# Loading the last rows of wo: the last 16 partitions in two loads of their own, and b1 and b2 from SyncE's queue

## The chip, the cores and the metric

The kernel runs on one core of a Trainium2 chip. The metric is device time in microseconds (us) of one execution. One execution was also recorded by the hardware profiler; its rows are what the profile sections quote.

## The reference, cut to what matters

Two tokens (B = 2) of width 512 go through one decode step of attention with cached keys and values, and through a small MLP that gates the result. K and V hold 32 heads of 8192 positions of 128 values for each token, all in fp32.

```python
def _A_ref(x, k_cache, v_cache, wq, wo):        # attention
    q = (x @ wq).reshape(B, Sq, H, Dh).transpose(0, 2, 1, 3)
    scores = einsum("bhqd,bhkd->bhqk", q, k_cache) * (Dh ** -0.5)
    o = einsum("bhqk,bhkd->bhqd", softmax(scores), v_cache)
    return o.transpose(0, 2, 1, 3).reshape(B, Sq, H * Dh) @ wo

def _B_ref(x, w1, b1, w2, b2):                  # MLP, d_ff = 1376
    h = gelu(layernorm(x) @ w1 + b1)
    return h @ w2 + b2

xn = layernorm(x)
out = x + _A_ref(xn, k, v, wq, wo) * silu(_B_ref(xn, w1, b1, w2, b2))
```

## The kernel before

**Tiling.** K and V are streamed in 32 turns. A turn takes two heads, one in partitions 0 to 63 and one in 64 to 127; each partition holds 128 positions of 128 values, so one turn's K and one turn's V are 8 MB each. VectorE multiplies K by q (`scores_mul`, L524) and sums over the 128 values (`scores_sum`, L531), each in two halves; `max_rows` and `max_dve` find the maximum, ScalarE takes the exponentials (`exps`, L552), and TensorE multiplies by V (`weighted`, L575, 64 matmuls).

**Buffers and queues.** K has two buffers (`kb0`, `kb1`), V one (`vb`). All large loads go out from SyncE, through the helper `load` (L314), on one queue, in program order: w1, w2, wq, the two halves of the first K turn, then K and V in turns, each as soon as its buffer is free. The last V turn goes into `kb1`. ScalarE issues three small loads at the start: x (L337), b1 and b2 (L339).

**Order.** `Plan` records every operation with the keys it reads and writes, and gives each engine its instructions in the order of recording, with the semaphore waits that the keys need. Every load has a semaphore of its own name (the fourth argument of `load` is the list of keys that it writes). SyncE runs no arithmetic, so its instructions are the loads in order, each behind its waits.

**The head.** While w1, w2, wq and the first K land, x is normalized twice, the MLP runs (`mlp`: L410 and L412 for w1 and b1, L452 for w2, L459 and L462 for b2), then q is computed (L482), and copied to all partitions (L495, L497). SyncE waits for L482 before it loads the second K turn into `kb0`, where wq was. b1 is one row of 1376 values in partition 32, b2 one row of 512; L412 and L462 add them with a matmul from a row of ones. w1, w2, b1, b2 and all small tiles of the head lie in `vb`, which the first V load overwrites.

**The tail.** After the last V turn that uses `vb`, `wo` is loaded there in five pieces (L619 to L621). Partition p holds 32 rows of wo, row c being 2 KB; `WO_PIECES` cuts the rows at 0, 16, 24, 29, 31 and 32, so the pieces are 4096, 2048, 1280, 512 and 256 KB over all 128 partitions. Meanwhile the last turn is finished, and `on`, the normalized attention output, is made. Then TensorE contracts: rows 0 to 23 with a 512 wide matmul each into `wide` (L648), which ScalarE copies out (L651); rows 24 to 28 with four 128 wide matmuls each into `acc` (L657, `rows(WIDE, FOLD)`); four matmuls that fold `wide` into `acc` (L662); rows 29 to 31 like 24 to 28 (`rows(FOLD, OC)`). A matmul of row c waits for the piece that holds it (`piece(c)`). `acc` is multiplied by the gate (L666), x is added (L667), and SyncE stores 4 KB (L668). WIDE is 24, FOLD 29, OC 32.

An fp32 matmul shows in the profile as two entries, each with its weight load.

Of the kernel before, what the change touches and what calls it, by code (L numbers as in the profile page):

```python
# [21 lines left out]
class Plan:  # L22
# [18 lines left out]
    def op(self, eng, fn, r=(), w=(), over=(), it=None, loop=False, dma=None):  # L41


        o = Op()
        o.eng, o.fn, o.it, o.loop, o.dma, o.tell = eng, fn, it, loop, dma, False
        need = {}

        def after(d, war):
            if d.dma is None and dma is None and d.eng == eng and (eng == "pe" or war):
                return  # L50
            if d.dma is None:
                if need.get(d.eng) is None or need[d.eng].idx < d.idx:
                    need[d.eng] = d
            else:
                k = ("dma", d.dma)
                if need.get(k) is None or need[k].idx < d.idx:
                    need[k] = d

        for k in r:
            if k in self.writer:  # L60
                after(self.writer[k], False)
        for k in list(w) + list(over):
            if k in self.writer:
                after(self.writer[k], False)
            for d in self.readers.get(k, ()):
                after(d, True)
        clock = self.clock[eng]
        need = {k: d for k, d in need.items() if clock.get(k, 0) < d.idx}
        o.deps = [(k, d) for k, d in need.items()
                  if not any(e is not d and e.done.get(k, 0) >= d.idx for e in need.values())]  # L70
        for _, d in o.deps:
            for k, v in d.done.items():
                clock[k] = max(clock.get(k, 0), v)
        own = eng if dma is None else ("dma", dma)
        self.count[own] = o.idx = self.count.get(own, 0) + 1
        o.done = dict(clock)
        o.done[own] = o.idx
        for k in w:
            self.writer[k] = o
            self.readers[k] = []  # L80
        for k in r:
            if k not in w:
                self.readers.setdefault(k, []).append(o)
        self.ops.append(o)
# [80 lines left out]
def decode_kernel(nc, x, kc, vc, wq, wo, w1, b1, w2, b2, out):  # L165
    P = 128
# [19 lines left out]
    OC = DH // PH  # L186
# [10 lines left out]
    op = plan.op  # L197

    def pe(fn, r=(), w=(), it=None, loop=False):
        op("pe", fn, r, w, it=it, loop=loop)  # L200
# [10 lines left out]
    def sbuf(name, shape):  # L211
        return nc.alloc_sbuf_tensor(name, shape, F32).ap()

    def psum(name, shape):
        return nc.alloc_psum_tensor(name, shape, F32).ap()
# [5 lines left out]
    vb = sbuf("vb", [P, KP * DH])  # L221
# [3 lines left out]
    wo_sb = vb.rearrange("p (c n) -> p c n", c=OC)  # L225
# [30 lines left out]
    on = sbuf("on", [P, RM, OC])  # L256
# [5 lines left out]
    def take(name, p, n, base=0, at=None):  # L262

        if at is None:
            at = used[0]
            used[0] += n
            assert used[0] <= KP * DH
        boot.append(name)
        return vb[base:base + p, at:at + n]
# [7 lines left out]
    b1_sb = take("b1", 1, F, R, at)  # L277
    b2_sb = take("b2", 1, D, R, at + F)
# [18 lines left out]
    acc = psum("acc", [P, P])  # L297
# [5 lines left out]
    def bank():  # L303
        i = turn[0] % 4
        turn[0] += 1
        return scratch[i], f"s{i}"
# [6 lines left out]
    def load(dst, src, sem, w, over=()):  # L313
        op("sp", lambda: nc.sync.dma_start(dst, src), (), w, over=over, dma=sem)  # L314

    def load_k(n):
        i = (n + 1) % 2
        if n in (0, N - 1):
            for s in range(2):
                load(kbuf[i][:, s * M:(s + 1) * M], kf[n][:, s * M:(s + 1) * M], f"k{i}{s}", [("kb", i, s)])  # L320
            return
        load(kbuf[i], kf[n], f"kb{i}", [("kb", i, s) for s in range(2)])
# [2 lines left out]
    WO_PIECES = (0, 16, 24, 29, 31, 32)  # L325
    WIDE, FOLD = WO_PIECES[-4:-2]


    load(w1_sb, w1.rearrange("(p c) f -> p c f", p=P), "w1", ["w1"])
    load(w2_sb, w2.rearrange("f n -> (f n)").rearrange("(p e) -> p e", p=P), "w2", ["w2"])  # L330
    load(wq_sb, wq.rearrange("(p c) n -> p c n", p=P), "wq", [("kb", 0, s) for s in range(2)])
    load_k(0)

# [1 line left out]
    dve(lambda: nc.vector.memset(eps_t, EPS), w=["eps"])  # L335
    act(lambda: nc.scalar.activation(warm, eps_t, AF.Sqrt), ["eps"], ["warm"])
    op("act", lambda: nc.scalar.dma_start(x_sb, x.rearrange("b s d -> (b s) d")), w=["x"], dma="x")  # L337
    for t, src, k in ((b1_sb, b1, "b1"), (b2_sb, b2, "b2")):
        op("act", lambda t=t, src=src: nc.scalar.dma_start(  # L339
            t.rearrange("o (k e) -> o k e", k=16), src.rearrange("(o k e) -> o k e", o=1, k=16)), w=[k], dma=k)  # L340


    pool(lambda: nc.gpsimd.memset(ident, 0.0), w=["ident"])
# [37 lines left out]
    for j in range(QT):  # L381
        pe(lambda j=j: matmul(px[R * j:R * j + RM, :P], pick, x_sb[:, j * P:(j + 1) * P],
                              start=True, stop=True), ["pick", "x"], [kx])
# [92 lines left out]
    for i in range(NQ):  # L476
        for c in range(ND):
            wv = wq_sb[:, c, :].rearrange("p (h s d) -> p h s d", s=U, d=DH)
            a = (NQ - 1 - i) * B
            for j in range(QT):  # L480
# [4 lines left out]
                    start=(i + c == 0), stop=(i == NQ - 1 and c == ND - 1)),  # L485
                   ["xnT"] + [("kb", 0, s) for s in range(2)], ["po"])
    act(lambda: nc.scalar.copy(q_nat, PO), ["po"], ["o4"])
    for k in range(N // NB):

        b, e = divmod(k, HH // NB)  # L490
        i, g = divmod(e, GQ)
        p, kp = bank()
        for s in range(U):
            a = R * (U * g + s) + B * i + b
            pe(lambda p=p, s=s, a=a: matmul(p[HP * s:HP * (s + 1), :], ident[:, a:a + 1].to_broadcast([P, HP]), q_nat,  # L495
                                            start=True, stop=True), ["ident", "o4"], [kp])
# [121 lines left out]

    wo_r = wo.rearrange("(p c) n -> p c n", p=P)  # L619
    for i, (a, e) in enumerate(zip(WO_PIECES, WO_PIECES[1:])):  # L620
        load(wo_sb[:, a:e], wo_r[:, a:e], f"wo{i}", [("wo", i)], over=["vb"])  # L621

    max_dve(N - 1)
    exps(N - 1)
# [17 lines left out]
    def piece(c):  # L642
        return ("wo", max(i for i, a in enumerate(WO_PIECES[:-1]) if a <= c))


    for c in range(WIDE):
        j = c % QT
        pe(lambda c=c, j=j: matmul(wide[R * j:R * j + RM, :], on[:, :, c], wo_sb[:, c, :],  # L648
                                   start=(c < QT), stop=(c + QT >= WIDE)), ["on", piece(c)], ["wide"])
# [4 lines left out]
    def rows(lo, hi):  # L654
        for c in range(lo, hi):
            for j in range(QT):
                pe(lambda c=c, j=j: matmul(acc[R * j:R * j + RM, :], on[:, :, c], wo_sb[:, c, j * P:(j + 1) * P],  # L657
                                           start=(c == WIDE), stop=(c == OC - 1)), ["on", piece(c)], ["acc"])

    rows(WIDE, FOLD)  # L660
    for j in range(QT):
        pe(lambda j=j: matmul(acc[R * j:R * j + RM, :], mod[:, :RM], w4[:, j * P:(j + 1) * P], start=False, stop=False),  # L662
           ["mod", "o4"], ["acc"])
    rows(FOLD, OC)

    dve(lambda: nc.vector.tensor_mul(gate, acc, gate), ["acc", "gate"], ["gate"])  # L666
# [30 lines left out]
```

## Time and profile before

| | us |
|---|---|
| median of 3 runs | 1300.4 (1300.06 to 1300.45) |
| profiled execution, its time | 1300.03 |
| profiled execution, span from first to last instruction | 1298.2 |
| VectorE busy in the span | 1134.6 (87%) |
| TensorE matmul busy in the span | 404.8 (31%) |
| DMA, mean over the span | 431 GB/s |
| TensorE clock granted, mean | 0.635 |

A core has 16 DMA engines. The DMA share of a window is the mean busy share of these 16. "issue to landing" runs from the start of SyncE's (or ScalarE's) issuing instruction to the last byte's notice on the load's semaphore. In the chain of waits each row is a start, a length and the work that the next row waited for; in the timeline a row is a start, a length, engine, line, operation, tiles and count, with the idle time before it in brackets. SPq and ACTq are the queues of SyncE and ScalarE, PEld is TensorE's weight load.

### The profile page before, as it was taken

The page shows a single profiled execution, that of the slowest core. Times are in us where ns is not written, and L with a number is a line of the kernel's source. Part 1 is how long each engine was busy: PE and PEld are TensorE (multiplying, and loading weights), DVE is VectorE, ACT ScalarE, POOL GpSimd, SP SyncE. Part 2 cuts the span into 40 slices and gives each one's busy share as a digit, 9 for nine tenths or more (in the row PEclk, how much of TensorE's full clock was granted, in tenths as well). Part 3 has the DMA queues.
Part 4 walks back from the last instruction along what each step waited for, and adds up shares of the span by engine and source line. Part 5 has one row for each costly group of instructions (what it writes and reads, how often), then busy time and mean ns, then how long its engine had stood idle before and what let it go on. Part 6 is the DMA issues. An engine that isn't in the chain of part 4 may idle for free.

```text
span 1298.2 us, 6788 instructions
## 1 busy us (share of the span) xinstructions
PE 404.8 (31%) x2728; PEld 123.9 (10%) x2728; DVE 1134.6 (87%) x276; ACT 77.6 (6%) x250; POOL 1.4 (0%) x8
## 2 busy tenths in 40 slices
PE   5602333312333312333321333321233321233337
PEld 1100011000101000101000101100001000001103
DVE  3599999888889988889988888988888988888991
ACT  1100000000000000000000000000000000000000
POOL 0000000000000000000000000000000000000000
PEclk9856666556666656666656666656666655666658
DMA  9999999999999999999999999999999999999998
GB/s 406 445 423 440 430 432 436 426 444 428 438 430 432 438 426 440 430 434 434 428 442 428 438 430 430 440 426 440 430 434 434 430 438 430 438 430 430 427 433 363
DMA packets 10826, 559.39 MB, mean 431 GB/s; under 512 B 1208, under 2 KB 1216, under 8 KB 1476
## 3 DMA queue, kind: packets, MB, share of 16 engines
q1 hardware_dynamic: 10812, 559.29, 99.7%
q8 instruction: 4, 0.07, 0.0%
q14 instruction: 2, 0.02, 0.0%
q10 hardware_dynamic: 8, 0.01, 0.0%
HBM read 559.30 MB, written 0.00 MB: 431 GB/s over the span
## 4 chain that ended last, share of the span: by engine, by line
DMA 74%; PE 24%; DVE 1%; issue 0%; ACT 0%; SPq 0%; DVEq 0%
DMA vb<-in_A_v_cache_dram 72%; PE po L575 22%; DMA vb<-in_A_wo_dram 2%; PE s L410 1%; PE po L482 1%; PE s L452 0%; PE s L412 0%; PE acc L657 0%; DVE vb L418 0%; ACT L431 0%; DVE vb L356 0%; PE s L459 0%; SPq L314 0%; DVE vb L367 0%; DVE vb L444 0%
## 5 line engine op out<-in xcount | busy, mean ns | idle before, releaser
L524 DVE TENSOR_TENSOR kb<-kb,Q 128x8192 f32<-128x8192 f32 x64 | 555.5, 8681 | 105.2 <-DMA kb<-in_A_k_cache_dram 95.9
L531 DVE TENSOR_REDUCE sc<-kb 128x64 f32<-128x8192 f32 x64 | 552.3, 8665 | 0.0
L575 PE MATMUL po<-vb,PZ 128*8 128x512 f32 x1984 | 280.7, 730 | 292.8 <-DMA vb<-in_A_v_cache_dram 292.8
L547 PE MATMUL s<-nm,srow 1*128 1x2 f32 x64 | 18.7, 359 | 364.0 <-DVE nm L541 364.0
L575 PEld LDWEIGHTS po<-vb,PZ 128*8 128x8 f32 x1984 | 56.4, 103 | 491.0 <-issue 489.5
L538 PE MATMUL s<-ident,mx 128*1 128x128 f32 x32 | 11.8, 369 | 192.7 <-DVE mx L535 192.7
L547 PEld LDWEIGHTS s<-nm,srow 1*128 1x128 f32 x64 | 15.9, 307 | 373.3 <-DVE nm L541 373.3
L582 ACT COPY o<-po 128x512 f32<-128x512 f32 x32 | 18.7, 585 | 533.3 <-PE po L575 533.3
L548 ACT COPY bias<-s 128x2 f32<-128x2 f32 x32 | 5.1, 160 | 622.1 <-PE s L547 622.1
L584 PE MATMUL s<-mod,o 128*128 128x2 f32 x256 | 33.6, 253 | 22.1 <-ACT o L582 22.1
L584 PEld LDWEIGHTS s<-mod,o 128*128 128x128 f32 x256 | 31.0, 191 | 51.3 <-ACT o L582 51.3
L552 ACT ACTIVATE PZ<-sc,bias 64x128 f32<-64x128 f32 x64 | 25.5, 399 | 1.8
L538 PEld LDWEIGHTS s<-ident,mx 128*1 128x1 f32 x32 | 2.5, 79 | 196.2 <-DVE mx L535 165.7
L590 DVE TENSOR_TENSOR Z<-blk,s 128x8 f32 (+1 forms) x32 | 5.2, 163 | 13.3 <-PE s L584 13.3
L418 DVE COPY vb<-vb 2x384 f32<-2x384 f32 x4 | 1.8, 500 | 15.9 <-ACT vb L414 15.9
L410 PE MATMUL s<-vb 128*2 128x512 f32 (+1 forms) x24 | 12.5, 673 | 0.3 <-ACT vb L375 0.3
L552 ACT ACTIVATION_READ_ACCUMULATOR PZ<-sc,bias 64x1 f32 x64 | 11.8, 185 | 0.0
L666 DVE TENSOR_TENSOR gate<-acc,gate 128x128 f32<-128x128 f32 x1 | 0.3, 291 | 12.1 <-PE acc L657 12.1
L535 DVE TENSOR_REDUCE mx<-sc 128x1 f32<-128x128 f32 x32 | 9.2, 286 | 1.1
L556 ACT ACTIVATE ZR<-half,rs 128x8 f32 (+1 forms) x32 | 9.6, 301 | 4.1
L575 PE MATMUL po<-kb,PZ 128*8 128x512 f32 x64 | 9.4, 755 | 1.4 <-ACT PZ L552 1.4
L541 DVE TENSOR_REDUCE nm<-s 1x2 f32<-1x128 f32 x32 | 8.7, 272 | 0.3 <-PE s L538 0.3
(88 smaller groups left out, 84.5 us busy)
## 6 DMA issues: line engine op xcount, KB each, us to landing
kb<-in_A_k_cache_dram SPq DMA_DIRECT2D x4, 4096.0 KB, 43.5
kb<-in_A_v_cache_dram SPq DMA_DIRECT2D x2, 4096.0 KB, 40.9
vb<-in_B_w_dram SPq DMA_DIRECT2D x2, 2752.0 KB, 12.5
vb<-in_A_wo_dram SPq DMA_DIRECT2D x1, 4096.0 KB, 19.0
vb<-in_A_wo_dram SPq DMA_DIRECT2D x1, 2048.0 KB, 23.5
vb<-in_A_wo_dram SPq DMA_DIRECT2D x1, 1280.0 KB, 26.1
vb<-in_A_wo_dram SPq DMA_DIRECT2D x1, 512.0 KB, 26.9
vb<-in_A_v_cache_dram SPq DMA_DIRECT2D x31, 29.5
```

The costliest lines, as they stand in the source:

```text
L410: pe(lambda f=f, w=w, ph=ph, c=c: matmul(ph[:B, :w], yT[:, c, :], w1_sb[:, c, f:f + w], start=(c == 0), stop=False), ["yT", "w1"], [k])
L482: pe(lambda i=i, c=c, wv=wv, a=a, j=j, hd=hd: matmul(PO[R * j:R * j + NQ * B, :].rearrange("m (h d) -> m h d", d=DH), xnT[:, c, a:a + NQ * ...
L524: vector(n, n, lambda n: nc.vector.tensor_tensor(out=k, in0=k, in1=cols(Q, n * DH, DH).unsqueeze(1).to_broadcast([P, M, DH]), op=ALU.mult) ...
L531: vector(n, n, lambda n: nc.vector.tensor_reduce(out=SC[:, s * M:(s + 1) * M], in_=k, axis=AX.X, op=ALU.add), [("kb", i, s)], [("sc", s)])
L535: vector(n, n, lambda n: nc.vector.tensor_reduce(out=MX, in_=SC, axis=AX.X, op=ALU.max), [("sc", 0), ("sc", 1)], ["mx"])
L538: pe(lambda i: transpose(PM[:1, :P], MX, ident), ["mx", "ident"], ["s1"], it=n, loop=n > 0)
L547: pe(lambda i: matmul(PN[:, :U], srow, NM, start=True, stop=True), ["srow", "nm"], ["s2"], **one)
L552: act(lambda i, r=r, s=s: nc.scalar.activation(PZ[r, :, s, :], sc[r], AF.Exp, bias=BIAS[r, s:s + 1], scale=SCALE, accum_out=RS[r]), ["bias ...
L556: act(lambda i: nc.scalar.activation(cols(ZR, i * UP - UP, UP), half, AF.Copy, scale=RS), ["half"] + [("rs", s) for s in range(U)], [("ZR" ...
L575: pe(lambda i, t=t, j=j, v=v: matmul(PO[R * j:R * j + U * JW, :], PZ[:, t].rearrange("p s j -> p (s j)"), v[:, t * JW:(t + 1) * JW, :].rea ...
L582: act(lambda i: nc.scalar.copy(O4, PO), ["po"], ["o4"], **one)
L584: pe(lambda i, k=k: matmul(PT[:, :U], O4[:, k * DH:(k + 1) * DH], mod[:, k:U * JW:JW], start=(k == 0), stop=(k == JW - 1)), ["o4", "mod"], ...
```

## The change

Rows 29 to 31 of wo (768 KB) are no longer loaded as two pieces over 128 partitions. Partitions 112 to 119 and 120 to 127 get a load each with all three rows (6 KB a partition, 48 KB a load), ahead of the two pieces, and the pieces then cover partitions 0 to 111 (448 and 224 KB). The matmuls of rows 29 to 31 wait for the two new loads as well as for their piece. The loads of b1 and b2 move from ScalarE's queue to SyncE's, behind w2 and ahead of wq.

```diff
+    PL = P - 16
     load(w1_sb, ...)
     load(w2_sb, ...)
+    for t, src, k in ((b1_sb, b1, "b1"), (b2_sb, b2, "b2")):
+        load(t.rearrange("o (k e) -> o k e", k=16), src.rearrange("(o k e) -> o k e", o=1, k=16), k, [k])
     load(wq_sb, ...)
     load_k(0)
...
     op("act", lambda: nc.scalar.dma_start(x_sb, x.rearrange("b s d -> (b s) d")), w=["x"], dma="x")
-    for t, src, k in ((b1_sb, b1, "b1"), (b2_sb, b2, "b2")):
-        op("act", lambda t=t, src=src: nc.scalar.dma_start(
-            t.rearrange("o (k e) -> o k e", k=16), src.rearrange("(o k e) -> o k e", o=1, k=16)), w=[k], dma=k)
...
     for i, (a, e) in enumerate(zip(WO_PIECES, WO_PIECES[1:])):
-        load(wo_sb[:, a:e], wo_r[:, a:e], f"wo{i}", [("wo", i)], over=["vb"])
+        if a < FOLD:
+            load(wo_sb[:, a:e], wo_r[:, a:e], f"wo{i}", [("wo", i)], over=["vb"])
+            continue
+        if a == FOLD:
+            for p in range(PL, P, 8):
+                load(wo_sb[p:p + 8, a:], wo_r[p:p + 8, a:], f"wol{p}", [("wol", p)], over=["vb"])
+        load(wo_sb[:PL, a:e], wo_r[:PL, a:e], f"wo{i}", [("wo", i)], over=["vb"])
...
-                 ... ["on", piece(c)], ["acc"])
+                 ... ["on", piece(c)] + ([("wol", p) for p in range(PL, P, 8)] if c >= FOLD else []), ["acc"])
```

More of the change, by code (lines that the diff above doesn't have):

```diff
@@ L657, in rows @@
                 pe(lambda c=c, j=j: matmul(acc[R * j:R * j + RM, :], on[:, :, c], wo_sb[:, c, j * P:(j + 1) * P],
-                                           start=(c == WIDE), stop=(c == OC - 1)), ["on", piece(c)], ["acc"])
+                                           start=(c == WIDE), stop=(c == OC - 1)), ["on", piece(c)] + ([("wol", p) for p in range(PL, P, 8)] if c >= FOLD else []), ["acc"])
     rows(WIDE, FOLD)
```

## The prediction

> **What bounds the kernel now.** I read the page's header and DMA part first, then the DMA issues with their landings, then the busy time by windows, and last the chain of waits at both ends.
>
> ```profile
> DMA 74%; PE 24%; DVE 1%; issue 0%; ACT 0%; SPq 0%; DVEq 0%
> ```
> ```profile
> q1 hardware_dynamic: 10812, 559.29, 99.7%
> q8 instruction: 4, 0.07, 0.0%
> ...
> q10 hardware_dynamic: 8, 0.01, 0.0%
> HBM read 559.30 MB, written 0.00 MB: 431 GB/s over the span
> ```
> ```profile
> 100.00:1200.00 1100.00, 314.82 (x2145) 95.93 (x2137) 1002.68 (x202) 57.39 (x197) 0.00 (x0) 0.62 1.00 434
> ```
>
> The chain by engines is three quarters DMA. SyncE's queue (q1) holds 99.7% of the 16 engines' span, and from 100 to 1200 us the DMA share is 1.00 at 434 GB/s (last two numbers of the window). So the kernel is one gapless stream of 559 MB, or 27.1 GB/s for each of 16 engines. VectorE, at 1003 of 1100 us, has spare time in every turn. A change that adds no bytes can touch only what stands before the stream and behind it.
>
> The tail is where the stream ends. The wo loads' landings come from these rows, the timeline's issues and the page's times to landing:
>
> ```profile
> 1266.34 2.23 SPq L314 DMA_DIRECT2D vb<-in_A_wo_dram  x5
> ```
> ```profile
> vb<-in_A_wo_dram SPq DMA_DIRECT2D x1, 4096.0 KB, 19.0
> vb<-in_A_wo_dram SPq DMA_DIRECT2D x1, 2048.0 KB, 23.5
> vb<-in_A_wo_dram SPq DMA_DIRECT2D x1, 1280.0 KB, 26.1
> vb<-in_A_wo_dram SPq DMA_DIRECT2D x1, 512.0 KB, 26.9
> ```
> ```profile
> vb<-in_A_wo_dram SPq DMA_DIRECT2D x1, 256.0 KB, 27.1
> ```
> ```profile
> 1266.34 0.33 SPq L314
> ...
> 1267.20 26.14 DMA vb<-in_A_wo_dram
> 1293.34 0.04 issue
> 1293.38 1.31 PE acc L657 x34
> 1294.70 0.22 PE acc L662 x7
> 1294.91 0.83 PE acc L657 x23
> 1295.75 0.02 issue
> 1295.77 0.30 DVE gate L666
> ```
>
> Five issues take 2.23 us, so the fourth and fifth start near 1267.7 and 1268.1; with 26.9 and 27.1 us the pieces land at 1294.6 and 1295.2. The chain is released by the third piece (rows 24 to 28, 1267.20 + 26.14 = 1293.34), and from there TensorE is busy nearly without a break to 1295.75. How near shows in the timeline of the same place:
>
> ```profile
> 1294.64 0.44 PEld L657 LDWEIGHTS acc<-vb,on 128*17 128x17 f32 x16
> 1294.72 0.99 PE L657 MATMUL acc<-vb,on 128*17 128x128 f32 x24
> 1295.27 0.18 PEld L657 LDWEIGHTS acc<-vb,on 128*17 128x17 f32 x8 [0.19 <-DMA vb<-in_A_wo_dram]
> ...
> 1296.42 0.70 SPq L668 DMA_DIRECT2D out_dram<-gate  x1
> ```
>
> Rows 29 and 30 load their weights from 1294.64, done at 1295.08; row 31 then stands 0.19 us idle for the last piece. So an earlier end of the stream pays at most 0.19 us, a later one pays in full.
>
> How evenly do the 16 engines finish? The last windows show it:
>
> ```profile
> 1293.25:1293.50 0.25, 0.12 (x4) 0.12 (x8) 0.00 (x0) 0.00 (x0) 0.00 (x0) 1.00 0.58 221
> 1293.50:1293.75 0.25, 0.25 (x13) 0.25 (x16) 0.00 (x0) 0.00 (x0) 0.00 (x0) 1.00 0.49 197
> 1293.75:1294.00 0.25, 0.25 (x20) 0.25 (x15) 0.00 (x0) 0.00 (x0) 0.00 (x0) 1.00 0.36 139
> 1294.00:1294.25 0.25, 0.25 (x20) 0.25 (x13) 0.00 (x0) 0.00 (x0) 0.00 (x0) 1.00 0.28 107
> ...
> 1294.50:1294.75 0.25, 0.25 (x19) 0.24 (x14) 0.00 (x0) 0.00 (x0) 0.00 (x0) 1.00 0.09 33
> ```
>
> At 1293.25 about nine of sixteen engines are still at work (0.58 x 16), at 1294.0 to 1294.25 four or five, at the end one or two. They are ragged by 1.5 us. No view names the engines.
>
> **The change part by part.** I make the sum against the profiled execution (1300.03 us; its span 1298.2 and 1.83 outside it) and add 0.37 to stand at the median of the runs, 1300.4.
>
> *Bytes per engine in the last three rows.* A piece over 128 partitions gives each engine 8 of them: 75 SyncE loads of 16 x (8 + 1) packets are 10800, and the store's 12 make the 10812 of q1. Over 112 partitions I take 7 each. For small loads the nearest row is q10's: x has two rows, b1 and b2 one each, and 8 packets fit x on two engines (2 rows, 2 end marks) and b1 and b2 on one each (1 and 1). So a load of 8 partitions goes out on 8 engines, one partition each. If both take the same eight, these carry 9 partitions of 6 KB and the others 7. 6 KB at 27.1 GB/s is 0.23 us: eight engines end 0.23 later, eight 0.23 earlier.
>
> [...]
>
> *What it does to the end.* If the last engine is among the eight with 9: row 31 waits until 1295.2 + 0.23, the end moves by +0.23. The piece with rows 29 and 30 would come 2 x 0.23 - 4 KB/27.1 (0.15) = 0.30 later, at 1294.9; its 16 weight loads (0.44) end near 1295.4, just ahead of row 31's data, so nothing more. If the last engine is among the eight with 7: its data come 0.23 earlier, and TensorE can use 0.19, unless a late engine of the other eight, four of which are late altogether, now takes the last place. Range of this term: -0.19 to +0.23.
>
> *Crowded writes.* Eight engines write into eight neighbouring partitions at once, which no row shows. Lower bound 0 (the pieces of 128 partitions run at full rate with as many engines). Upper bound: all sixteen partitions at one engine's rate, 96 KB / 27.1 GB/s = 3.6 us in place of 0.46, so +3.2 on the eight engines. I take 0, by the row of the stream that it is nearest to.
>
> *Issues and waits in the tail.* Two more issues from SyncE at 2.23 / 5 = 0.45 us put the last at 1269.5 in place of 1268.6; the first piece lands at 1285.3, so 16 us of queued data hide them. Uncovered they would cost 0.9. TensorE gets two more waits ahead of row 29, already met by then; the gaps marked issue in the chain are 0.02 to 0.04, so below 0.1 and inside the 0.19 idle. Behind them stand all of rows 29 to 31, for which L666 waits.
>
> *b1 and b2 in the head.*
>
> ```profile
> 1.47 0.53 ACTq L339 DMA_DIRECT2D vb<-in_B_b_dram  x2
> 1.65 0.43 SPq L314 DMA_DIRECT2D kb<-in_A_wq_dram  x1
> ...
> 2.12 44.65 SPq L314 DMA_DIRECT2D kb<-in_A_k_cache_dram  x3
> ...
> 17.02 1.01 PE L412 MATMUL s<-vb,ones 1*2 1x512 f32 x2
> ...
> 39.34 7.05 PE L482 MATMUL po<-kb,vb 128*4 128x512 f32 x64
> ```
> ```profile
> vb<-in_B_w_dram SPq DMA_DIRECT2D x1, 2752.0 KB, 15.5
> ```
> ```profile
> kb<-in_A_k_cache_dram SPq DMA_DIRECT2D x1, 4096.0 KB, 53.4
> ```
> ```profile
> 0.73 1.28 ACT L336 ACT_TABLE_LOAD   x1 [0.73 <-PEq L684]
> ```
>
> ScalarE's two issues (0.53 us) end at 2.00, under its table load, which ends at 2.01: their removal gives 0. On SyncE two issues of 0.27 to 0.45 us delay wq and the first K by 0.5 to 0.9 us. w1 and w2 are queued by then, and w2 (issued at 1.2, the second of two) lands at 16.7, so 13 us of data hide it. b1 now lands behind w2: 5.4 KB at 27.1 GB/s, 0.20 us, on an engine that no longer carries b1 and b2 ahead of w2's end (7.4 KB, 0.28 us). So b1 lands by 16.9 at the latest, and L412 reaches it at 17.02. I take 0. If it were late by the whole time from the store's issue (1296.42) to the end (1298.2), 1.8 us, it would land at 18.5 and TensorE would stall 1.5 us; L482 and SyncE's wait for it, which releases the second K load, slide as much. The second half of the first K, issued before 3.4 and 53.4 us under way, lands at 55.5 or later, 9 us after that load's issue (the third of its row, ending at 2.12 + 44.65 = 46.8). Cover holds; uncovered 1.5 us.
>
> **The sum**: -0.19 or +0.23 from the balance, 0 to 0.1 from waits, 0 from the rest. With both signs about as likely and the loss the larger, I take +0.1: 1300.03 + 0.1 + 0.37 = **1300.5 us**.
>
> **The rivals.**
>
> 1. *The lighter engines hold the last byte.* The forecast with the other sign, 1300.2. For it: only four or five engines are late, and they may all sit there. Against: one of four in the heavier half caps it.
> 2. *Nothing is shifted*, because the second small load takes the other eight engines: every engine keeps 8 partitions, 1300.4. For it: no row shows the engines of a small load.
> 3. *Crowded writes decide.* In full they cost 0.2 + 3.2: 1300.4 + 3.4 = 1303.8, slower by 0.26%. It passes 0.2% (2.6 us) if the 96 KB go below 96 / (2.6 - 0.23 + 0.46) = 35 GB/s together. Two partition groups in parallel give about 1302. Against: eight engines move 217 GB/s in the stream.
> 4. *Each small load holds the queue by itself.* The store shows 1.8 us for 4 KB from issue to end; two such spans give 1300.4 + 3.6 = 1304.0. Against: the last wo piece (256 KB) lands 0.6 us behind the one before, which is its bytes at 433 GB/s with no fixed time. [...]
> 5. *Instruction fetch in the tail.*
>
> ```profile
> 1294.25:1294.50 0.25, 0.25 (x17) 0.25 (x12) 0.00 (x0) 0.00 (x0) 0.00 (x0) 1.00 0.55 147
> ```
>
> The share rises again to 0.55 here, between 0.28 and 0.09: one of q8's four packets of 16 KB. With other instruction counts it can fall on an engine that still loads wo: 16 KB at 27.1 GB/s is 0.6 us, more if it is slow. 1301.0 to 1301.6.
> 6. *b1 late and the cover gone*: 1300.4 + 1.5 = 1301.9.
>
> **How the numbers follow.** Within 0.2% (2.6 us) a measurement of this kernel can't be told from no change; the three runs lie 0.39 apart. Forecast (heavier engines last) 0.39, rival 1 0.30, rival 2 0.10, rival 3 mild (about 1302) 0.06 and in full 0.02, rival 4 0.03, rival 5 0.05, rival 6 0.02. That leaves 0.03 for a cause of a gain that I don't see. Same: 0.39 + 0.30 + 0.10 + 0.06 + 0.05 + 0.02 = 0.92; slower 0.02 + 0.03 = 0.05; faster 0.03. The range takes in rivals 1 and 2 and most of 5, with the runs' scatter at both ends: 1299.9 to 1301.5. Outside are 0.02, 0.03 and 0.03 of both ends, rival 6, rival 3 mild and a little of 5, 0.17.
>
> **What would show it.** Right: q1 at 10816 packets with the loads of 48 KB on eight engines each (two pieces of 16 x 8, two loads of 16, and 4 for b1 and b2, in place of two of 144); the last landing moved by 0.2 us either way; the third piece landing unmoved against the end of V; L412 starting within 0.1 us of 17.0 and L482 within 0.2 of 39.3; the windows of the middle still at 434 GB/s. Wrong: a last piece that lands over 1 us later against the third piece (rivals 3 to 5), an idle row of L412 released by a DMA that is seen again at the issue of the second K load, or a share below 0.95 near 17 us.

## The result and the profile after

The changed kernel takes 1302.68 us (median of 22 runs, 1301.41 to 1303.56) where the kernel before takes 1300.13 (22 runs, 1300.03 to 1300.45): a ratio of 1.0017, 95% interval 1.0012 to 1.0023. It is slower by 2.55 us, just below the 0.2% that was named beforehand as indistinguishable, and outside the range of the prediction. The scatter has grown too, from 0.4 us to 2.1. The profiled execution took 1301.8 us, with a span of 1300.4.

The time divides into two parts that moved in opposite directions. Over the runs, the span rose from 1298.2 to 1301.3 us (medians of 33 runs of the kernel before and 22 of the changed one), and the time outside the span fell from 1.83 (1.87 beside the later runs) to 1.34: +3.1 - 0.5 = +2.6. The 22 spans of the changed kernel lie in two groups, ten from 1300.1 to 1300.9 us and twelve from 1301.3 to 1302.2. The profiled execution is of the shorter group, 2.2 us above the kernel before.

Page of the changed kernel, its DMA queues:

```profile
q1 hardware_dynamic: 10816, 559.30, 99.6%
q8 instruction: 4, 0.07, 0.0%
q14 instruction: 3, 0.02, 0.0%
q10 hardware_dynamic: 4, 0.00, 0.0%
```

q1 has the 10816 packets that the prediction counted: each small load is 8 packets of 6 KB and 8 end marks of 4 bytes, where a load over 128 partitions has 16 end marks. Eight engines for the one and sixteen for the other are the author's reading of these counts; no view names the engines. q14, which had two packets in the span before, has three; that row will matter below.

Windows of the changed kernel (the last two numbers are DMA share and GB/s):

```profile
100.00:1200.00 1100.00, 319.55 (x2153) 96.35 (x2141) 1001.61 (x202) 57.36 (x197) 0.00 (x0) 0.61 1.00 434
```
```profile
1292.00:1293.00 1.00, 0.39 (x4) 0.00 (x0) 0.00 (x0) 0.56 (x1) 0.00 (x0) 1.00 0.94 195
1293.00:1294.00 1.00, 0.00 (x0) 0.00 (x0) 0.00 (x0) 0.03 (x1) 0.00 (x0) 1.00 1.02 203
1294.00:1295.00 1.00, 0.00 (x0) 0.00 (x0) 0.00 (x0) 0.00 (x0) 0.00 (x0) 1.00 0.79 150
```

The same first window of the kernel before:

```profile
1292.00:1293.00 1.00, 0.23 (x4) 0.00 (x0) 0.00 (x0) 0.58 (x1) 0.00 (x0) 1.00 0.98 389
```

The middle of the run is unchanged, 434 GB/s. In the tail the engines are as busy as before (0.94 against 0.98) and move half the bytes (195 against 389 GB/s). A busy share alone would have shown nothing: for the same 10 KB a packet takes about twice as long (720 to 960 ns in place of 389, below). Chain of waits of the changed kernel, its end:

```profile
1266.06 29.52 DMA vb<-in_A_wo_dram
1295.57 0.04 issue
1295.62 1.32 PE acc L665 x40
1296.94 0.22 PE acc L670 x8
1297.15 0.80 PE acc L665 x24
```

The piece that released TensorE before releases it now as well, the third one, rows 24 to 28 over all 128 partitions, which the change does not touch. It lands at 1295.57 in place of 1293.34, 2.2 us late. After it TensorE works without a break. The loads behind it, that is those that were changed, no longer stop anything:

```profile
vb<-in_A_wo_dram SPq DMA_DIRECT2D x1, 224.0 KB, 29.4
```

Issued near 1268.0, the last piece lands near 1297.4, 1.8 us behind the third, nearly as before (1.9, from 1293.3 to 1295.2).

The kept trace records the size and the duration of every DMA packet, and in the tail the sizes tell the loads apart: a packet of rows 24 to 28 has 10 KB, one of the two small loads 6 KB. Packets of rows 24 to 28 that start between 1289 and 1291 us take 385 to 394 ns in the changed kernel. The first packet of a small load starts at 1291.34, and the six packets of rows 24 to 28 that start after 1292 take 720 to 960 ns. In the kernel before, the five that start after 1292 take 389 to 393. So the last packets of the unchanged piece are slowed while packets of the new loads are on their way.

The head of the changed kernel, from its timeline:

```profile
16.30 1.01 PE L413 MATMUL s<-vb,ones 1*2 1x512 f32 x2 [0.39 <-DMA vb<-in_B_b_dram]
...
45.06 0.33 SPq L314 DMA_DIRECT2D kb<-in_A_k_cache_dram  x1
```

L413 (L412 before) waited 0.39 us for b1, because the matmuls ahead of it were through earlier in this execution (at 15.9, where L412 started at 17.0 before). This varies without the change too: in e4 below, whose head is that of the kernel before, the same line starts at 15.65. The load that hangs on this chain went out earlier than before (45.1 against 46.4), into a queue that was full.

### The profile page after: what moved, and what is told of

The parts are those of the page before. It is cut to its first block, busy times and chain, and to the rows that moved or that the text cites. A ratio compares the mean times of both kernels' runs of the same rounds, so it can differ in the third digit from the quotient of the medians.

```text
span 1300.4 us, 6791 instructions
## 1 busy us (share of the span) xinstructions
PE 407.2 (31%) x2728; PEld 123.9 (10%) x2728; DVE 1134.7 (87%) x276; ACT 77.6 (6%) x250; POOL 1.4 (0%) x8
## 3 DMA queue, kind: packets, MB, share of 16 engines
q1 hardware_dynamic: 10816, 559.30, 99.6%
## 4 chain that ended last, share of the span: by engine, by line
DMA 75%; PE 24%; issue 0%; DVE 0%; ACT 0%; SPq 0%
DMA vb<-in_A_v_cache_dram 71%; PE po L576 22%; DMA vb<-in_A_wo_dram 2%; DMA vb<-in_B_b_dram 1%; PE po L483 1%; PE s L411 0%; PE s L453 0%; PE s L413 0%; PE acc L665 0%; SPq L314 0%; DVE vb L419 0%; ACT L432 0%; PE s L425 0%; PE s L460 0%; DVE vb L445 0%
## 5 line engine op out<-in xcount | busy, mean ns | idle before, releaser
L576 PE MATMUL po<-vb,PZ 128*8 128x512 f32 x1984 | 284.5, 738 | 296.1 <-DMA vb<-in_A_v_cache_dram 296.1
```

The lines of the kernel that those rows point to most:

```text
L576: pe(lambda i, t=t, j=j, v=v: matmul(PO[R * j:R * j + U * JW, :], PZ[:, t].rearrange("p s j -> p (s j)"), v[:, t * JW:(t + 1) * JW, :].rea ...
```

## The experiments

Theory C: the loss lies in the tail, in the wo loads, and the head costs nothing. Within it, theory S blames the two loads of 8 neighbouring partitions, rival M the two pieces over 112 partitions. Each run is compared with the kernel before on the same chip (1300.05 to 1300.08 there). The spans given are medians over the timed runs, to be held against 1298.2 of the kernel before (1298.3 beside e9, which ran on another chip).

**e1_bias_only.** The head part alone.

```diff
+    for t, src, k in ((b1_sb, b1, "b1"), (b2_sb, b2, "b2")):
+        load(..., k, [k])            # SyncE, behind w2
-        op("act", ... nc.scalar.dma_start(...), w=[k], dma=k)
```

> b1 and b2 on SyncE's queue alone, the wo loads as in the kernel before. Theory C (crowding in the tail costs all of the 2.5 us): 1300.1, within 0.3 of the kernel before, third wo piece landing 2.0 us after... no later than 1293.5. Rival H (the head costs part of it): 1300.6 to 1302.5.

Measured: 1299.56 us (1299.39 to 1299.82; the kernel before 1299.86 to 1300.31), ratio 0.9997, interval 0.9988 to 1.0006. Span 1298.1. The head costs nothing, which theory C wanted, and there is a gain of 0.49 us that neither expected. The interval of the ratio includes no change, but the two sets of runs hardly come within 0.04 us of each other. All of it lies outside the span: 1.33 in place of 1.83.

**e2_split_only.** The wo split of the change, with b1 and b2 on ScalarE's queue as before.

> The wo split alone, b1 and b2 on ScalarE's queue. Theory C: all of the change's loss, 1302 to 1303.3, with a DMA rate of 160 to 240 GB/s in the last 3 us of the loads. Rival H: clearly less than the change, below 1301.5.

Measured: 1302.71 us (1301.63 to 1303.56), ratio 1.0021, interval 1.0012 to 1.0030, span 1301.4. All of the span's loss comes from the split. Its windows from 1292 to 1295 us show 211, 182 and 131 GB/s. Time outside the span is 1.35 here too, although ScalarE loads b1 and b2.

**e3_112_only.** No small loads: the last 16 partitions of rows 29 to 31 are left out.

```diff
-        load(wo_sb[:, a:e], wo_r[:, a:e], ...)
+        n = P if a < FOLD else P - 16
+        load(wo_sb[:n, a:e], wo_r[:n, a:e], ...)
```

> Rows 29 to 31 over partitions 0 to 111 as two pieces, the last 16 partitions of these rows not loaded, so 96 KB less is read and the product lacks them. Theory S (the loads of 8 neighbouring partitions crowd the writes): no loss, 1299.8 to 1300.1. Rival M (pieces over 112 partitions, 7 for each engine, are themselves slow): 1301 to 1302.5, with the rate of these two pieces at about half of 433 GB/s.

Measured: 1303.01 us (1301.47 to 1303.46), ratio 1.0020, interval 1.0011 to 1.0029, span 1301.1. Theory S falls as the only cause: with 96 KB less to load and no small load at all, the kernel is as slow as the whole change, and above both expectations. Window of e3:

```profile
1292.00:1293.00 1.00, 0.29 (x4) 0.00 (x0) 0.00 (x0) 0.58 (x1) 0.00 (x0) 1.00 0.88 197
```

Not all of this loss is the loads'. In the profiled execution of e3 the third piece lands at 1295.40, 2.1 us late, but the span is 3.1 us longer. The rest is TensorE, whose last matmuls take 3.4 us (1295.45 to 1298.81) in place of 2.4, because its granted clock (the third number from the end) falls to 0.50. The same window of e3 and of the changed kernel, whose profiled execution keeps 1.00 to its last matmul:

```profile
1296.50:1297.00 0.50, 0.50 (x16) 0.47 (x12) 0.00 (x0) 0.00 (x0) 0.00 (x0) 0.50 0.11 33
```
```profile
1296.50:1297.00 0.50, 0.50 (x28) 0.45 (x24) 0.00 (x0) 0.00 (x0) 0.00 (x0) 1.00 0.08 29
```

Such a fall, between 1295.4 and 1296.3 us, stands in the profiled executions of e3, e6, e7 and e9 and, ahead of the last matmul, in none of the others. In the kernel before TensorE is through at 1295.75; a piece that lands 2 us late moves its work to where the clock can fall. The late piece is the effect that all slow kernels share, so the table below has a column for it.

**e4_small_beside.** The five pieces as before, the two small loads in addition, into `kb0`. SyncE issues them at 1268.0, when `kb0` is free; their packets start at 1291.2, so this wait is hidden. As in the change, the matmuls of rows 29 to 31 wait for them (not printed, likewise in e5 and e6).

```diff
+        if a == FOLD:
+            for p in range(P - 16, P, 8):
+                load(spare[p:p + 8, a:], wo_r[p:p + 8, a:], f"wol{p}", ...)
         load(wo_sb[:, a:e], wo_r[:, a:e], ...)
```

> All five pieces over 128 partitions as before, and ahead of the fourth the two loads of 8 neighbouring partitions again, into a free buffer in the same partitions, so 96 KB more are read. Theory S: 1302 to 1303 and a third piece that lands 1 to 2 us late. Rival M: only the bytes, +0.2 to +0.5, 1300.3 to 1300.6.

Measured: 1301.51 us (1300.78 to 1302.37), ratio 1.0011, interval 1.0002 to 1.0020, span 1300.2. The time lies between the two expectations. So rival M is not the only cause either: the small loads alone cost 2.0 us of span, and the third piece lands late here too. Chain of e4:

```profile
1265.81 28.75 DMA vb<-in_A_wo_dram
1294.56 0.04 issue
```

What e3 and e4 have in common is that their loads cover other groups of partitions than a load over 128. That the cost hangs on this, on the side of the writing, is theory P of e5, e6, e7 and e9. It is a guess of the author's, which held e5 to be the cheap arrangement and e6 and e9 to be dear ones; which engine writes which partition no view shows.

**e5_small_low** and **e6_small_high.** As e4, with other partitions.

```diff
-                load(spare[p:p + 8, a:], wo_r[p:p + 8, a:], ...)          # 112 to 119, 120 to 127
+                rows8 = slice(base + p, base + 32, 4)                     # base 0 (e5) or 64 (e6), p = 0, 1
+                load(spare[rows8, a:], wo_r[rows8, a:], ...)
```

> As e4 (five pieces over 128 partitions, and two loads of 8 partitions beside them into a free buffer, 96 KB more), but the 8 partitions lie 4 apart: 0, 4 to 28, then 1, 5 to 29. [...] Rival Q (any small load, or any load on half of the engines, costs as e4's did): span 1299.5 to 1301.

> [...] Rival Q: as e4, 1299.5 to 1301. Rival N (only neighbouring partitions crowd): as e5, 1298.2 to 1298.8.

Measured: e5 1299.86 us (1299.73 to 1300.39), ratio 0.9998, interval 0.9989 to 1.0007, span 1298.5; e6 1300.92 us (1300.59 to 1302.12), ratio 1.0008, interval 0.9999 to 1.0017, span 1299.6. The bytes, the number of loads and of packets (10844 in q1) and the spacing are the same; only the partitions differ, with the rows of wo that belong to them, and so does the cost: +0.3 us of span for e5, about what 96 KB take at 433 GB/s (0.23), and +1.4 for e6. In e6's profiled execution the third piece is 0.9 us late, and the clock falls as in e3. The same window of e5, then of e6:

```profile
1292.00:1293.00 1.00, 0.24 (x4) 0.00 (x0) 0.00 (x0) 0.58 (x1) 0.00 (x0) 1.00 1.02 410
```
```profile
1292.00:1293.00 1.00, 0.28 (x4) 0.00 (x0) 0.00 (x0) 0.58 (x1) 0.00 (x0) 1.00 1.02 291
```

Both have all engines busy (1.02); e5 keeps the full rate (410 GB/s, where the kernel before has 389), e6 loses a quarter or more (291). The packets of rows 24 to 28 that start after 1292 take 387 to 399 ns in e5, as in the kernel before, and 516 to 661 in e6; worked out from the two windows, 10 KB take 0.41 and 0.57 us on the mean. Small loads as such (rival Q) and neighbours alone (rival N) are out. Whether neighbours add something to e4 (1300.2 against e6's 1299.6) stays open, as the runs overlap. That the piece ahead of the small loads is on time in e5 shows in its timeline at TensorE's start on rows 24 to 28 (1293.38 before):

```profile
1293.39 1.32 PE L662 MATMUL acc<-vb,on 128*17 128x128 f32 x40 [1.16 <-DMA vb<-in_A_wo_dram]
```

**e7_112_linear.** As e3, read from one contiguous stretch.

```diff
-        load(wo_sb[:n, a:e], wo_r[:n, a:e], ...)
+        load(wo_sb[:n, a:e].rearrange("p c n -> p (c n)"),
+             wo.rearrange("k n -> (k n)")[:n * m].rearrange("(p e) -> p e", e=m), ...)   # m = (e - a) * 512
```

> As e3 (two pieces over 112 partitions, 96 KB not loaded), but read from one contiguous stretch of wo instead of rows 64 KB apart, so rows 29 to 31 of the product hold other rows of wo. Theory P (the cost is on the writing side): as e3, span 1299.6 to 1301.6, median near 1301. Rival R (the cost is in reading rows 64 KB apart in another grouping): span 1298.0 to 1298.6.

Measured: 1302.26 us (1301.43 to 1303.38), ratio 1.0017, interval 1.0008 to 1.0026, span 1300.4 (1299.5 to 1301.5). The loss does not hang on reading rows 64 KB apart; this may have a part of it, as e3's median span is 0.7 higher, but the ranges overlap. A run that keeps e5's rows of wo and writes them to e6's partitions was not made, so a part of the reading side is not excluded. Window of e7:

```profile
1292.00:1293.00 1.00, 0.18 (x4) 0.00 (x0) 0.00 (x0) 0.58 (x1) 0.00 (x0) 1.00 0.98 215
```

**e8_sync_pad.** This one asks about e1's 0.49 us. Outside the span the kernel before has one more packet, of 8 KB, seen in a window from 1298.3 to 1301 us, behind its last instruction:

```profile
q14 instruction: 1, 0.01, 0.7%
```

The kernels with a shorter time outside (e1, e2, e4 and the changed one) have two more loads on SyncE and their third q14 packet in the span; e3, with SyncE's program as before, has 1.83 us outside and the packet behind its end. So the length of SyncE's program is suspected, and lengthened alone.

```diff
+    for _ in range(8):
+        op("sp", lambda: nc.sync.nop())      # behind the last wo load
```

> The kernel before with eight empty instructions on SyncE behind the last wo load, b1 and b2 on ScalarE's queue. Theory I (e1's 0.49 us is an 8 KB instruction block of SyncE that was fetched after the last instruction and, with a longer program of SyncE, is fetched during the run): 1299.6, with three q14 packets in the span and the span unmoved at 1298.2. Rival B (the gain comes from taking b1 and b2 off ScalarE's queue): 1300.05.

Measured: 1299.45 us (1299.40 to 1299.52), where the kernel before has 1299.88 to 1300.37: no overlap, ratio 0.9995, interval 0.9986 to 1.0004. Span 1298.1, 1.34 outside. Rival B is out: b1 and b2 stay on ScalarE here. The page of e8 has four q14 packets in the span where three were expected; two of them stand before 60 us and 90 us as in the kernel before, one is the block in question, seen in a window from 1260 to 1275 us,

```profile
q14 instruction: 1, 0.01, 0.1%
```

and the fourth is a packet of 88 bytes at 0.1 us that in the other runs falls ahead of the span. This is the lowest median of the study, below both kernels that were compared.

**e9_halves.** Rows 29 to 31 over all partitions, in halves of 64, no small load.

```diff
-        load(wo_sb[:, a:e], wo_r[:, a:e], ...)
+        for g in range(2):
+            r = slice(64 * g, 64 * (g + 1))
+            load(wo_sb[r, a:e], wo_r[r, a:e], f"wo{i}{g}", [("wo", i, g)], over=["vb"])
```

> Rows 29 to 31 in two pieces as before, but each piece as two loads of 64 partitions (0 to 63, 64 to 127), 4 partitions to an engine, no small loads; the same bytes, evenly spread. [...] Rival U (the cost is the uneven or odd number of partitions to an engine, 7 and 1): span 1298.0 to 1298.6; with two more SyncE loads, time 1299.5 to 1299.9.

Measured: 1302.63 us (1301.62 to 1303.74), ratio 1.0020, interval 1.0011 to 1.0029, span 1301.3. q1 has 10844 packets here, 4 x (64 + 16) in place of 2 x 144; read like the counts above, that is sixteen engines for each half and 4 partitions to an engine. By this reading rival U falls: the same bytes, the same share for each engine, even numbers, and as slow as the change. The third piece lands 2.0 us late; in the profiled execution the rest of the loss is the clock, as in e3. Window and chain of e9:

```profile
1292.00:1293.00 1.00, 0.26 (x4) 0.00 (x0) 0.00 (x0) 0.58 (x1) 0.00 (x0) 1.00 0.94 152
```
```profile
1267.04 28.28 DMA vb<-in_A_wo_dram
1295.32 0.04 issue
```

The last column is TensorE's start on rows 24 to 28 in the profiled execution, which the third piece releases.

| kernel | us | span | outside | rows 24 to 28 |
|---|---|---|---|---|
| before | 1300.05 to 1300.13 | 1298.2 to 1298.3 | 1.83 to 1.87 | 1293.38 |
| changed | 1302.68 | 1301.3 | 1.34 | 1295.62 |
| e1 head only | 1299.56 | 1298.1 | 1.33 | 1293.39 |
| e2 split only | 1302.71 | 1301.4 | 1.35 | 1295.48 |
| e3 112 partitions, no small loads | 1303.01 | 1301.1 | 1.83 | 1295.45 |
| e4 small loads 112 to 127 beside | 1301.51 | 1300.2 | 1.36 | 1294.61 |
| e5 small loads 0, 4 ... beside | 1299.86 | 1298.5 | 1.34 | 1293.39 |
| e6 small loads 64, 68 ... beside | 1300.92 | 1299.6 | 1.33 | 1294.25 |
| e7 as e3, contiguous source | 1302.26 | 1300.4 | 1.88 | 1294.89 |
| e8 eight empty SyncE instructions | 1299.45 | 1298.1 | 1.34 | 1293.40 |
| e9 halves of 64 | 1302.63 | 1301.3 | 1.34 | 1295.36 |

## Why the prediction was wrong

**The step that failed** is "Crowded writes": "I take 0, by the row of the stream that it is nearest to." The row was of loads over 128 partitions, 8 to each engine by the packet counts, and e3, e4, e6 and e9 show that it does not bound a load with another arrangement. In place of 0 the runs showed +3.1 us of span, of which the profiled execution has 2.2, all of it a third piece that lands late. The upper bound of that step (+3.2) was about the size, but from another mechanism: it let two small loads crawl at one engine's rate (27.1 GB/s), where the windows show the whole stream at half its rate (195 GB/s in place of 389), and e3 shows it without any small load (197).

**The pieces over 112 partitions** were costed by their bytes alone ("Over 112 partitions I take 7 each"). They bring the full loss by themselves (e3, +2.9), and the small loads bring 2.0 by themselves (e4). The two do not add up: in the changed kernel, with both, the stream runs at 150 to 203 GB/s for 3 us, and the third piece lands within 0.2 us of e3's (1295.57 and 1295.40). That both slow the same packets would explain it and was not tried.

**Where it lands** was wrong with it. The third piece was to land unmoved, and the sign of trouble was to be a last piece over 1 us later against the third. The distance stayed near 1.9 us, and the third piece came 2.2 us late. The engines finish up to 1.5 us apart, as the prediction read from the last windows. Packets of the new loads therefore start (1291.34) while packets of rows 24 to 28 are still to come, and these then take 720 to 960 ns in place of 389. The prediction had no term for a load that slows the one ahead of it. Rival 3 was the nearest in kind (crowded writes), though that the engines meet in the writing is not shown; with a chance of 0.08 it was held far too low.

**The balance term** (-0.19 or +0.23) can't be seen below 3 us of other effects. It assumes that both small loads go out on the same eight engines, which no run shows. Of the kernels here only e5 has two such loads and an undisturbed stream, and its +0.3 is about its bytes.

**The head** was right where it was argued: b1 and b2 cost the span nothing (e1: 1298.1), b1 was there at 16.3, in e1 at 16.9 (by 16.9, it was said), and the slack of the queue in front of the second K load covered the 0.39 us that TensorE waited. Two signs named beforehand were missed to the early side, the start of L412 (16.30, not 17.0) and of L482 (37.95, not 39.3); the starts differ by as much between kernels with the same head, so they could not have told.

**The time outside the span** was taken as fixed at 1.83 us. It fell by 0.5 with SyncE's longer program (e8). Rival 5 looked for instruction fetches in the tail, but only as a packet in the way of wo, not as one behind the end.

**Rival 4**, two spans of 1.8 us for the small loads, is refuted by e5: two such loads with their bytes cost 0.3 us.

## What to carry to other kernels

When a stream runs at its limit over 128 partitions, as this one at 434 GB/s, try to keep every load of it over 128 partitions. Loads over 112 (e3 197, e7 215 GB/s from 1292 to 1293 us), two halves of 64 (e9, 152) and loads of 8 partitions in the upper half (e4 295, e6 291) slowed this one, where the kernel before has 389, and the load ahead of them paid; loads of 8 partitions between 0 and 29 (e5, 410) did not slow it. Read DMA share and GB/s together: in the changed kernel a share of 0.94 at 195 GB/s went with packets of 10 KB that took 720 to 960 ns in place of 389. Where a late load leads into TensorE work, look at the granted clock before putting all of the loss down to the load: in e3 it fell to 0.50, and the last matmuls took 3.4 us in place of 2.4. And where the time moves but the span does not, look at the instruction packets behind the last instruction before crediting the edit.

## What the runs showed of the hardware that was not expected

**Which partitions a load covers mattered more here than how many bytes it has.** e5 and e6 differ only in partitions (and the rows of wo that belong to them) and cost 0.3 and 1.4 us of span; e9, with every engine at its old share by the packet counts, costs 3.0. Loads of 8 partitions were cheap in 0, 4 to 28 and 1, 5 to 29 (410 GB/s from 1292 to 1293 us) and dear in 64, 68 to 92 and 65, 69 to 93 (291), and with halves of 64 partitions the stream ran at 152 GB/s there, in place of 389. Why these partitions and not those is not shown. That the engines meet on the writing side, as theory P guessed, is supported by e7 (another order of reading, still 1302.26) but not shown; which engine carries a packet, and which partitions it writes, are not seen in any view.

**An instruction block behind the end.** The kernel before fetches 8 KB after its last instruction. The kernels with two q14 packets in their span have 1.83 to 1.88 us outside it (the kernel before and e3, where a third is seen behind the end, and e7), those with three or four 1.33 to 1.36. Eight empty instructions on SyncE bring it into the run and save 0.5 us. That the block is SyncE's is concluded from e8, where nothing else was changed; why a longer program fetches it earlier is not shown.

**Open.** The kernels with a disturbed tail scatter by 1.5 to 2.1 us from run to run (e9: 1301.62 to 1303.74), the others by 0.1 to 0.7. One part can be TensorE's clock: its fall costs e3 and e9 about 1 us of their profiled executions and the changed kernel's nothing, and the two groups of the changed kernel's spans lie about 1 us apart. Another part may come from how far apart the engines finish (1.5 us in the kernel before), which is a guess. Neither was tried.
